# Scores of two attention units in one TensorE stretch, and four PSUM banks for x @ w_in

## Chip, core and metric

One core of a Trainium2 chip runs the whole program in one launch. The metric is the device time in microseconds; the comparison is by the median of several runs.

## The reference

Sliding-window attention with sink tokens, followed by a feed-forward layer with a gate. q, k and v have 4 batches, 8 heads, 768 positions and 64 columns a head. All inputs and the output are float32.

```python
scores = scale * np.matmul(q, k.transpose(0, 1, 3, 2))
keep = is_sink | in_window          # key < 4, or 0 <= query - key < 128
scores = np.where(keep, scores, -1000000000.0)
a = np.exp(scores - max); a = a / (np.sum(a) + 1e-09)
attn = np.matmul(a, v)
x = attn.transpose(0, 2, 1, 3).reshape(3072, 512)
h = x @ w_in                        # 512 -> 2048
g = h * (1.0 / (1.0 + np.exp(-beta * h)))
out = g @ w_out                     # 2048 -> 512
```

## The kernel before

**Attention.** The work is cut into 32 *units*: a unit n is two heads (a pair of heads, 64 columns each, so that both fill the 128 partitions) and half of the 768 queries (384 of them). Four units in a row give one tile of 384 tokens of x, so there are 8 tiles T. `place(n)` gives batch, pair of heads, half, and the buffer set `pb`, which is n % 4. A unit goes through: loads of q, k, v (SP's queue), casts to bf16 (POOL), turning q and k (for units from `XBAR` = 12 on by a DMA transpose on SP's queue, earlier by TensorE), for the second half the sink scores (`scores_sink`, L533 and L536), the scores (TensorE), the exponential (ScalarE), a multiplication with the mask (VectorE), A.V (`attend`, TensorE, L636 and L647, into bank `av`), the normalisation (`normalise`, VectorE, L656 and L658), and the turning of the result into `xT` (`transpose_out`, for units from 12 on a DMA transpose, L667).

Scores are only taken where the window lets something through: six blocks of 128 x 128 per head and unit (`BLOCKS`). The two heads lie in the two halves of the partitions, so each score matmul uses 64 rows of the array, and a matmul of head 0 and one of head 1 run side by side. In units from 12 on `scores_at_once` (L597) takes all six blocks of both heads in one group, head 0 into banks `s0` and `s1`, head 1 into `tr` and `av` (the four banks of `s_ps`); one ScalarE instruction (L604) takes the exponential of all 1536 columns into `E[n % 2]`, one VectorE instruction (L613) masks it.

**Feed-forward.** For each tile T there are 16 groups i of x @ w_in (`hidden`, L695: four matmuls of 384 columns into one bank), each followed by a tanh on ScalarE (`tanh`, L703, into one of three buffers `th`) and by the gate on VectorE (`gate`, L717), which reads the same bank and th and writes `g`. `project` (L744) multiplies g with w_out: 48 matmuls of 512 columns a tile, in three accumulations of 16, into `acc0` and `acc1`, copied out by ScalarE (L752) and stored by SP (L759). `hidden_bank(i)` chooses the bank of a group: before, from i = `S_P0` = 32 on, it alternates between `h0` and `h1`. PSUM has eight banks: h0, h1, s0, s1, tr, av, acc0, acc1.

**Order.** The main loop walks steps s from -6 on. `FIRST[n]` is the step at which unit n starts, and `STEPS` says what happens so many steps later (0: in, 1: sink scores, 3: scores, 5: A.V, 7: out). `casts` and `loads` say at which step the casts and loads of later units are written. In a step there is one group of x @ w_in, three matmuls of w_out, and what the units have there. This program order only fixes who depends on whom: `Prog.order` then places all operations with a list scheduler that has a busy time and a latency for each operation, taking on each engine the one that can start first, and `Prog.emit` writes the order of each engine with the semaphore waits. `P.together` keeps a group of matmuls in one piece; `behind` makes an operation wait for an earlier operation of the same group. So the engines' order follows from the planner, not from the steps directly.

Of the kernel before, what the change touches and what calls it, by code (L numbers as in the profile page):

```python
# [5 lines left out]
F32 = mybir.dt.float32  # L6
AF = mybir.ActivationFunctionType
# [7 lines left out]
SCALE = 1.0 / (D ** 0.5)  # L15
D1 = D + 1

TT = 384
NT = NTOK // TT
NU = 4 * NT  # L20
NM = DF // 128
# [12 lines left out]
BLOCKS = (((0, 0), (0, 1), (0, 2), (2, 2), (1, 1), (1, 2)),  # L34
          ((2, 3), (3, 3), (3, 4), (5, 5), (4, 4), (4, 5)))
# [3 lines left out]
S_P0 = 2 * NM  # L39
# [1 line left out]
S_END = S_PIPE + (NT - 2) * NM  # L41

FIRST = {4: -6, 5: -4, 6: -2, 7: 1, 8: 26, 9: 30, 10: 34, 11: 38}
FIRST.update({12: 44, 13: 47, 14: 50, 15: 53})
FIRST.update({n: 42 + 4 * (n - 12) for n in range(16, NU)})

XBAR, WHOLE = 12, 16

ADDED, FAR = 5, -float(1 << 20)
STEPS = {0: "in", 1: "sink", 2: "a", 3: "b", 5: "av", 7: "out"}  # L50


# [226 lines left out]
def bass_streamingllm_window__then__act_swish_beta_kernel(  # L279
# [25 lines left out]
    def ps(name, shape, dtype):  # L305
        ctx.append(nc.psum_tensor(name, list(shape), dtype))
        return ctx[-1].__enter__()
# [31 lines left out]
    g = [sb(f"g{z}", (128, NM, TT), BF16) for z in range(2)]  # L339
    out_sb = [sb(f"out_sb{z}", (128, NOUT), F32) for z in range(4)]  # L340

    h_ps = ps("h_ps", (128, 2, 512), F32)
    s_ps = ps("s_ps", (128, 4, 512), F32)
    acc = [ps(f"acc{z}", (128, NOUT), F32) for z in range(2)]
    tr_ps, av_ps = s_ps[:, 2, :], s_ps[:, 3, :]

    P = Prog()
    op = P.op


    def pe(n):
        return {"busy": 2.5 + n / 2.4, "lag": 260.0}

    def act(n):
        return {"busy": 80.0 + 0.81 * n, "lag": 140.0}
# [56 lines left out]
    def place(n):  # L412

        return n // 8, n % 4, n // 4 % 2, n % 4
# [115 lines left out]

    def scores_sink(n, bank, name):
        pb = place(n)[3]
        op("pe", lambda e: e.matmul(bank[:, 0, 0:TT], k_sink[pb][:, :], qkT[pb][:, 1, 0, :],  # L533
                                    start=True, stop=True),
           r=[("k_sink", pb), ("qT", pb, 1)], w=[f"{name}0"], **pe(TT))
        op("act", lambda e: e.activation(E_sink[n % 2][:, :], bank[:, 0, 0:TT], AF.Exp, bias=0.0,  # L536
                                         scale=SCALE),
           x=[f"{name}0"], w=[("E_sink", n % 2)], **act(TT))

    def width(half, c):  # L540
        return 128 * sum(t[2] for t in CHUNKS[half][c])
# [41 lines left out]
    def scores_at_once(n):  # L583

        _, _, half, pb = place(n)
        pieces = []
        for x, (kb, qb) in enumerate(BLOCKS[half]):
            if x % 4 and pieces[-1][1] == kb:
                pieces[-1] = (*pieces[-1][:3], pieces[-1][3] + 1)
            else:  # L590
                pieces.append((x, kb, qb, 1))
        with P.together("pe"):
            for x, kb, qb, nq in pieces:
                for hh in range(2):
                    rows = slice(64 * hh, 64 * hh + 64)
                    bank, at = 2 * hh + x // 4, x % 4
                    op("pe", lambda e, kb=kb, bank=bank, qb=qb, at=at, nq=nq, rows=rows: e.matmul(  # L597
                        s_ps[:, bank, 128 * at:128 * (at + nq)],
                        qkT[pb][rows, kb // 3, 1, kb % 3 * 128:kb % 3 * 128 + 128],
                        qkT[pb][rows, half, 0, qb % 3 * 128:(qb % 3 + nq) * 128], start=True, stop=True),  # L600
                       r=[("qT", pb, half), ("qkT", pb, kb // 3)], w=[("s0", "s1", "tr", "av")[bank]],
                       busy=27.0 * nq + 20.0, lag=260.0)
        z = n % 2
        op("act", lambda e: e.activation(  # L604
            E[z][:, :, :, :].rearrange("p c h x -> p c (h x)"),
            s_ps[:, :, :].rearrange("p (h b) x -> p h (b x)", h=2)[:, :, 0:768], AF.Exp,
            bias=0.0, scale=SCALE),
           x=["s0", "s1", "tr", "av"], w=[("E", z, 0), ("E", z, 1)], **act(1536))

    def mask_at_once(n):  # L610
        z, half = n % 2, place(n)[2]
# [72 lines left out]
    def hidden_bank(i):  # L684


        k = i if i < 4 else i % 2 if i < NM else i % 4 if i < S_P0 else 3 - i % 2
        if k < 2:
            return acc[k][:, 0:TT], f"acc{k}"
        return h_ps[:, 3 - k, 0:TT], f"h{3 - k}"  # L690
# [170 lines left out]

    at = {16: 38, 17: 46, 18: 52, 19: 57, 24: 69, 25: 75, 26: 81, 27: 87}
    loads = {t + 2 * x: (n, name) for n, t in at.items() for x, name in enumerate("qkv")}
    casts = {FIRST[n - 2] + 1: n for n in range(6, NU) if n not in (8, 9)}
    for s in range(-6, S_END + NM):
        i = s if 4 <= s < S_P0 else s - NM if S_PIPE <= s < S_END else None
        if i is not None:
            done = hidden(i)
        here = [(n, STEPS[s - FIRST[n]]) for n in range(4, NU) if s - FIRST[n] in STEPS]
        later = []  # L870
        for n, step in here:
            half = place(n)[2]
            if step == "in" and n < XBAR:
                transpose_in(n, eng="dve")
            if step == "sink" and half == 1:
                scores_sink(n, *((h_ps, "h") if n < 8 else (s_ps, "s")))
            if step == "b" and n >= XBAR:
                scores_at_once(n)
                later.append(lambda n=n: mask_at_once(n))
            if step in ("a", "b") and n < XBAR:  # L880
                scores(n, "ab".index(step), *((h_ps, "h") if n < 8 and step == "b" else (s_ps, "s")))
                later.append(lambda n=n, step=step: mask(n, "ab".index(step)))
            if step == "av":
                ended = attend(n)
                later.append(lambda n=n: normalise(n))
                if n >= XBAR:
                    later.append(lambda n=n: transpose_out(n))
                if half == 0:
                    later.append(lambda n=n, ended=ended: sink_keys(n, ended))
            if step == "out":  # L890
                if n < XBAR:
                    transpose_out(n, eng="act" if n < 8 else "dve")
        if s in casts:
            n = casts[s]
            cast(n)
            if n in (12, 13):
                load(n + 2)
        if s == FIRST[5] + 2:
            for x in range(4, 8):
                cast_w(x)  # L900
            load(8)
            load(9)
            load(10)
            load(11)
            load_w(8)
            load_w(9)
            load_w(10)
            load_w(11)
            load_w(12)
            load_w(13)  # L910
            load_w(14)
            load_w(15)
            load(12)
            load(13)
        if s == 34:

            first = {0: (mask_a[:, :], MASK_A), 1: (mask_b[:, 128:512], MASK_B)}
            for half in range(2):
                op("gp", lambda e, half=half: e.tensor_copy(mask_all[:, half, 0:TT], first[half][0]),
                   r=[*first[half][1], ("v_aug", 3, 0)], w=[("mask_all", half, 0)], busy=300.0)  # L920
                for x, n in ((0, 1), (1, 2)):
                    at = TT + 128 * x
                    op("gp", lambda e, half=half, n=n, at=at: e.tensor_copy(
                        mask_all[:, half, at:at + 128 * n], mask_b[:, 0:128 * n]),
                       r=[*MASK_B, ("v_aug", 3, 0)], w=[("mask_all", half, 1)], busy=200.0)
        if s == FIRST[7] + 1:

            for x in (8, 9, 10, 11):
                cast_w(x)
            cast(8)  # L930
            cast_w(12)
            cast_w(13)
            cast(9)
            cast_w(14)
            cast_w(15)
        if S_P0 <= s < S_PIPE:

            for t, (bank, name, eng) in enumerate(
                    ((acc[0][:, :], "acc0", "act"), (acc[1][:, :], "acc1", "act"),
                     (h_ps[:, 1, :], "h1", "dve"))):  # L940
                done = project(0, t, s - S_P0, bank, name, eng)
        elif s >= S_PIPE:
            T = (s - S_PIPE) // NM + 1
            for x in range(3 * (s % NM), 3 * (s % NM) + 3):
                a = (3 * T + x // NM + 1) % 2
                if T == NT - 1 and x // NM == 2:
                    done = project_last(x % NM // 8, x % 8 * 2)
                    done = project_last(x % NM // 8, x % 8 * 2 + 1)
                    continue
                done = project(T, x // NM, x % NM, acc[a][:, :], f"acc{a}")  # L950
        if i is not None:
            gate(i)
        for fn in later:
            fn()
        if s in loads:
            load_whole(*loads[s], done)
# [39 lines left out]
```

## Time and profile before

| | |
|---|---|
| median of 3 runs | 229.04 us (228.92 to 229.59) |
| the profiled execution, its time | 229.57 us |
| its span, first to last instruction | 227.8 us |
| granted TensorE clock, mean | 0.999 |
| TensorE matmuls (PE) | 217.5 us busy, 1709 records |
| ScalarE (ACT) | 139.7 us busy |
| VectorE (DVE) | 135.8 us busy |
| GpSimd (POOL) | 76.7 us busy |
| w_out matmuls, 128x512 (L744 into acc) | 380 ns each, 329 records |
| w_in matmuls, 128x384 (L695 into h_ps) | 326 ns each, 424 records |
| exponential of a unit (L604) | 1444 ns, 20 of them |
| mask of a unit (L613) | 996 ns, 20 of them |
| tanh (L703), gate (L717) | 581 and 552 ns |

The profile tells of one execution. Matmuls are pipelined: the duration of a matmul (326 ns for 384 columns) is longer than the time from its start to the start of the next one, and it is the latter that adds up on TensorE. PEld are the weight loads of TensorE, which overlap its matmuls. In lists of groups and of waits, the time behind "<-" says what ended the idle time; "issue" is idle time for which the profile shows no releaser. L-numbers are lines of the kernel before, unless they are said to be of the changed one.

### The profile page before, as it was taken

To read this page: it belongs to the slowest core of one execution; us is meant where nothing else is said; L and a number is where in the kernel's file an instruction comes from. 1 tells how busy PE (TensorE), PEld (TensorE's weight loads), DVE (VectorE), ACT (ScalarE), POOL (GpSimd) and SP (SyncE) were. 2 spreads that over 40 slices of the span, in tenths; PEclk is the share of its full clock that TensorE was granted. 3 is DMA by queue.
4 is the path that set the end of the run, shared out by engine and by line. 5 is a ranking of instruction groups with operands and counts; after the bars stand their busy time and mean duration, and the time that the engine had idled before them with its cause. 6 is when DMAs were issued, how large, how long until landed. Compare 5 with 4: busy or idle time off the path is not lost.

```text
span 227.8 us, 4408 instructions
## 1 busy us (share of the span) xinstructions
PE 217.5 (95%) x1709; PEld 120.4 (53%) x1733; DVE 135.8 (60%) x261; ACT 139.7 (61%) x222; POOL 76.7 (34%) x149
## 2 busy tenths in 40 slices
PE   7897898999999999999999999999999999999995
PEld 4554555655445555444555555555555555555554
DVE  5657887798666656534677577656656555353300
ACT  2765987794436667536777676665676764555410
POOL 6877776798434130653204266000000000000000
PEclk9999999999999999999999999999999999999999
DMA  6999999996999989999999998501101101111022
GB/s 190 295 351 300 338 320 270 353 370 158 135 215 279 207 174 210 288 231 147 243 239 207 264 211 168 134 20 63 46 20 63 63 20 63 46 49 46 12 80 92
DMA packets 95436, 39.78 MB, mean 175 GB/s; under 512 B 81960, under 2 KB 88376, under 8 KB 95416
## 3 DMA queue, kind: packets, MB, share of 16 engines
q1 hardware_dynamic: 93760, 38.75, 67.5%
q10 hardware_dynamic: 1656, 0.76, 1.2%
q8 instruction: 13, 0.21, 0.4%
q14 instruction: 7, 0.06, 0.1%
HBM read 27.30 MB, written 6.29 MB: 147 GB/s over the span
## 4 chain that ended last, share of the span: by engine, by line
PE 88%; DVE 6%; DMA 2%; issue 1%; ACTq 1%; ACT 1%; DVEq 0%
PE acc L744 34%; PE h_ps L695 30%; PE s_ps L647 5%; PE acc L695 4%; PE s_ps L597 4%; DMA g<-in_v_dram 2%; DVE qkT L513 2%; PE s_ps L560 2%; PE h_ps L744 1%; DVE E L578 1%; PE s_ps L636 1%; PE s_ps L504 1%; DVE g L717 1%; DVE o_norm L658 1%; PE s_ps L533 1%
## 5 line engine op out<-in xcount | busy, mean ns | idle before, releaser
L744 PE MATMUL acc<-w_out,g 128*128 128x512 bf16 x329 | 89.3, 380 | 1.2 <-issue 0.3
L703 ACT ACTIVATE th<-h_ps,beta_half 128x384 f32<-128x384 f32 x106 | 60.5, 581 | 46.7 <-PE h_ps L695 43.8
L695 PE MATMUL h_ps<-xT,w_in 128*128 128x384 bf16 x424 | 82.2, 326 | 0.1
L717 DVE SCALAR_TENSOR_TENSOR g<-th,h_ps 128x384 bf16<-128x384 f32 x106 | 57.6, 552 | 39.8 <-ACT th L703 38.2
L695 PEld LDWEIGHTS h_ps<-xT,w_in 128*128 128x128 bf16 x424 | 40.5, 98 | 32.7 <-DVE g L717 1.8
L744 PEld LDWEIGHTS acc<-w_out,g 128*128 128x128 bf16 x352 | 32.1, 98 | 30.1 <-issue 3.7
L613 DVE TENSOR_TENSOR E<-E,mask_all 128x1536 bf16<-128x1536 bf16 x20 | 19.9, 996 | 18.6 <-ACT E L604 18.6
L604 ACT ACTIVATE E<-s_ps 128x1536 bf16<-128x1536 f32 x20 | 28.9, 1444 | 3.0 <-PE s_ps L597 2.9
L484 POOL CAST v_aug<-v_stage 128x384 bf16<-128x384 f32 x32 | 18.3, 586 | 29.6 <-PE s_ps L647 15.3
L481 POOL CAST qk<-q_stage 128x384 bf16<-128x384 f32 x32 | 18.2, 569 | 19.0 <-DMA q_stage<-in_q_dram 13.4
L481 POOL CAST qk<-k_stage 128x384 bf16<-128x384 f32 x31 | 17.7, 570 | 11.8 <-DMA k_stage<-in_k_dram 11.7
L647 PEld LDWEIGHTS s_ps<-v_aug,E 128*128 128x128 bf16 x384 | 17.1, 97 | 5.6 <-DVE E L613 0.7
L752 ACT ACTIVATE out_sb<-acc 128x512 f32<-128x512 f32 x22 | 13.0, 596 | 11.0 <-PE acc L744 10.6
L647 PE MATMUL s_ps<-v_aug,E 128*128 128x65 bf16 x384 | 19.3, 193 | 0.3 <-DVE E L578 0.3
L658 DVE TENSOR_TENSOR o_norm<-s_ps,rden 128x384 bf16<-128x384 f32 x32 | 17.8, 558 | 1.6
L567 ACT ACTIVATE E<-s_ps 128x768 bf16<-128x768 f32 x16 | 13.0, 810 | 9.2 <-PE s_ps L560 9.2
L695 PE MATMUL acc<-xT,w_in 128*128 128x384 bf16 x88 | 17.0, 327 | 1.2 <-DVE g L717 1.2
L703 ACT ACTIVATE th<-acc,beta_half 128x384 f32<-128x384 f32 x22 | 12.7, 583 | 6.0 <-PE acc L695 5.4
L717 DVE SCALAR_TENSOR_TENSOR g<-th,acc 128x384 bf16<-128x384 f32 x22 | 11.5, 549 | 3.1 <-ACT th L703 2.8
L695 PEld LDWEIGHTS acc<-xT,w_in 128*128 128x128 bf16 x88 | 7.9, 98 | 6.6 <-DVE g L717 2.0
L656 DVE RECIPROCAL rden<-s_ps 128x6 f32<-128x6 f32 x32 | 6.1, 191 | 7.0 <-PE s_ps L647 6.7
L597 PE MATMUL s_ps<-qkT 64*128 64x256 bf16 (+2 forms) x144 | 10.1, 254 | 0.0
(77 smaller groups left out, 158.9 us busy)
## 6 DMA issues: line engine op xcount, KB each, us to landing
out_dram<-out_sb SPq DMA_DIRECT2D x23, 256.0 KB, 2.4
wst<-in_moe_w_in_dram SPq DMA_DIRECT2D x8, 512.0 KB, 5.3
wst<-in_moe_w_out_dram SPq DMA_DIRECT2D x8, 512.0 KB, 9.0
q_stage<-in_q_dram SPq DMA_DIRECT2D x8, 384.0 KB, 4.1
k_stage<-in_k_dram SPq DMA_DIRECT2D x8, 384.0 KB, 3.9
v_stage<-in_v_dram SPq DMA_DIRECT2D x8, 384.0 KB, 3.8
v_stage<-in_v_dram SPq DMA_DIRECT2D x30, 96.0 KB, 4.6
q_stage<-in_q_dram SPq DMA_DIRECT2D x12, 192.0 KB, 5.1
```

The source lines that it names most:

```text
L481: op(eng, lambda e, x=x, name=name: e.tensor_copy(qk16[z][:, x, :, :, :], view(name)), r=[(name + "_stage", pb, half, hh) for hh in range( ...
L484: op("gp", lambda e: e.tensor_copy(v_aug[pb][:, 3 * half:3 * half + 3, :, 0:D], view("v")), r=[("v_stage", pb, half, hh) for hh in range(2 ...
L567: op("act", lambda e: e.activation(E[n % 2][:, c, :, 0:at], bank[:, 0:2, 0:at], AF.Exp, bias=0.0, scale=SCALE), x=[f"{name}0", f"{name}1"] ...
L597: op("pe", lambda e, kb=kb, bank=bank, qb=qb, at=at, nq=nq, rows=rows: e.matmul(s_ps[:, bank, 128 * at:128 * (at + nq)], qkT[pb][rows, kb ...
L604: op("act", lambda e: e.activation(E[z][:, :, :, :].rearrange("p c h x -> p c (h x)"), s_ps[:, :, :].rearrange("p (h b) x -> p h (b x)", h ...
L613: op("dve", lambda e: e.tensor_tensor(both, both, mask_all[:, half, :].unsqueeze(1).to_broadcast([128, 2, 768]), ALU.mult), r=[("E", z, 0) ...
L647: last=(x == len(kbs) - 1): e.matmul(av_ps[:, at + hh * D1:at + hh * D1 + D1], E[z][:, c, h2, col:col + 128], v_aug[pb][:, kb, hh, :], sta ...
L658: op("dve", lambda e: e.tensor_tensor(o_norm[o][:, :, :, :].rearrange("p m h d -> p (m h) d"), src[:, :, 0:D], rden[z][:, :].unsqueeze(2). ...
L695: return op("pe", lambda e: e.matmul(bank, w_in16[:, c, m * 128:(m + 1) * 128], xT[:, c, T * TT:(T + 1) * TT], start=(c == 0), stop=(c == 3)),
L703: op("act", lambda e: e.activation(th[i % 3][:, :], bank, AF.Tanh, bias=0.0, scale=beta_half[:, m:m + 1]), x=[name], r=["beta"], w=[("th", ...
L717: op("dve", lambda e: e.scalar_tensor_tensor(g[T % 2][:, m, :], th[i % 3][:, :], 1.0, bank, ALU.add, ALU.mult), r=[("th", i % 3)], x=[name ...
L744: node = op("pe", lambda e: e.matmul(bank, g[T % 2][:, m, t * 128:(t + 1) * 128], w_out16[:, m, :], start=(m == 0), stop=(m == NM - 1)), r ...
```

## The change

From unit 16 on (`PAIRED`) units n and n + 1, n even, take their scores in one group, `scores_pair`: the six banks h0, h1, s0, s1, tr, av are now one tensor `six`; unit n has av, h0, h1 and unit n + 1 has s0, s1, tr, each with 12 blocks of 128 columns in three banks without holes (before: 6 blocks in each pair of banks). The middle bank of the three holds blocks of both heads, and the first matmul of head 1 there is made to wait (`behind`) for the last one of head 0 there. The matmuls of both units and both heads are interleaved so that the columns given to each head stay even. Two exponentials and two masks follow. The A.V of the second unit comes `LATE` = 2 steps later, casts of odd units too; both units of a pair start at the same step, pairs 8 steps apart.

The groups of x @ w_in go round h0, h1, s0, s1 from i = 32 on (`TURN` = 0). In a step that holds sink scores or scores of a unit from 12 on, the gate is written ahead of them, since it still reads a bank that they may write. The sink scores of the second half go to `s0` for units 8 to 15 as before and to `tr` for units from 16 on.

```diff
@@ -41,12 +41,14 @@
 S_END = S_PIPE + (NT - 2) * NM
 
 FIRST = {4: -6, 5: -4, 6: -2, 7: 1, 8: 26, 9: 30, 10: 34, 11: 38}
-FIRST.update({12: 44, 13: 47, 14: 50, 15: 53})
-FIRST.update({n: 42 + 4 * (n - 12) for n in range(16, NU)})
+FIRST.update({12: 44, 13: 47, 14: 50, 15: 53, 16: 60, 17: 60})
+FIRST.update({n: 68 + 8 * (n // 2 - 9) for n in range(18, NU)})
+TURN = 0
 
 XBAR, WHOLE = 12, 16
 
 ADDED, FAR = 5, -float(1 << 20)
+LATE, PAIRED = 2, 16
 STEPS = {0: "in", 1: "sink", 2: "a", 3: "b", 5: "av", 7: "out"}
 
 
@@ -339,8 +341,8 @@
     g = [sb(f"g{z}", (128, NM, TT), BF16) for z in range(2)]
     out_sb = [sb(f"out_sb{z}", (128, NOUT), F32) for z in range(4)]
 
-    h_ps = ps("h_ps", (128, 2, 512), F32)
-    s_ps = ps("s_ps", (128, 4, 512), F32)
+    six = ps("six", (128, 6, 512), F32)
+    s_ps, h_ps = six[:, 0:4, :], six[:, 4:6, :]
     acc = [ps(f"acc{z}", (128, NOUT), F32) for z in range(2)]
     tr_ps, av_ps = s_ps[:, 2, :], s_ps[:, 3, :]
 
@@ -530,12 +532,12 @@
 
     def scores_sink(n, bank, name):
         pb = place(n)[3]
-        op("pe", lambda e: e.matmul(bank[:, 0, 0:TT], k_sink[pb][:, :], qkT[pb][:, 1, 0, :],
+        op("pe", lambda e: e.matmul(bank[:, 0:TT], k_sink[pb][:, :], qkT[pb][:, 1, 0, :],
                                     start=True, stop=True),
-           r=[("k_sink", pb), ("qT", pb, 1)], w=[f"{name}0"], **pe(TT))
-        op("act", lambda e: e.activation(E_sink[n % 2][:, :], bank[:, 0, 0:TT], AF.Exp, bias=0.0,
+           r=[("k_sink", pb), ("qT", pb, 1)], w=[name], **pe(TT))
+        op("act", lambda e: e.activation(E_sink[n % 2][:, :], bank[:, 0:TT], AF.Exp, bias=0.0,
                                          scale=SCALE),
-           x=[f"{name}0"], w=[("E_sink", n % 2)], **act(TT))
+           x=[name], w=[("E_sink", n % 2)], **act(TT))
 
     def width(half, c):
         return 128 * sum(t[2] for t in CHUNKS[half][c])
@@ -607,6 +609,46 @@
             bias=0.0, scale=SCALE),
            x=["s0", "s1", "tr", "av"], w=[("E", z, 0), ("E", z, 1)], **act(1536))
 
+    def scores_pair(n):
+
+        banks = {n: ("av", "h0", "h1"), n + 1: ("s0", "s1", "tr")}
+        with P.together("pe"):
+            runs = {0: [], 1: []}
+            for hh in range(2):
+                for bank in ((1, 0) if hh == 0 else (2, 1)):
+                    for u in banks:
+                        for x, (kb, qb) in enumerate(BLOCKS[place(u)[2]]):
+                            if (6 * hh + x) // 4 != bank:
+                                continue
+                            if runs[hh] and runs[hh][-1][:3] == [u, bank, kb]:
+                                runs[hh][-1][5] += 1
+                            else:
+                                runs[hh].append([u, bank, kb, qb, (6 * hh + x) % 4, 1])
+            columns, middle = [0, 0], {}
+            while runs[0] or runs[1]:
+                hh = 0 if runs[0] and (not runs[1] or columns[0] <= columns[1]) else 1
+                u, bank, kb, qb, at, nq = runs[hh].pop(0)
+                columns[hh] += nq
+                _, _, half, pb = place(u)
+                rows = slice(64 * hh, 64 * hh + 64)
+                op("pe", lambda e, kb=kb, bank=bank + (3 if u == n else 0), qb=qb, at=at, nq=nq, rows=rows,
+                   pb=pb, half=half: e.matmul(
+                    six[:, bank, 128 * at:128 * (at + nq)],
+                    qkT[pb][rows, kb // 3, 1, kb % 3 * 128:kb % 3 * 128 + 128],
+                    qkT[pb][rows, half, 0, qb % 3 * 128:(qb % 3 + nq) * 128], start=True, stop=True),
+                   r=[("qT", pb, half), ("qkT", pb, kb // 3)], w=[banks[u][bank]],
+                   behind=middle.pop(u, None) if (hh, bank) == (1, 1) else None,
+                   busy=27.0 * nq + 2.0, lag=260.0)
+                if (hh, bank) == (0, 1):
+                    middle[u] = len(P.group.items) - 1
+            P.group.busy += 200.0
+        for u, names in banks.items():
+            first = 3 if u == n else 0
+            op("act", lambda e, u=u, first=first: e.activation(
+                E[u % 2][:, :, :, :].rearrange("p c h x -> p (c h x)"),
+                six[:, first:first + 3, :].rearrange("p b x -> p (b x)"), AF.Exp, bias=0.0, scale=SCALE),
+               x=names, w=[("E", u % 2, 0), ("E", u % 2, 1)], **act(1536))
+
     def mask_at_once(n):
         z, half = n % 2, place(n)[2]
         both = E[z][:, :, :, :].rearrange("p c h x -> p c (h x)")
@@ -684,7 +726,10 @@
     def hidden_bank(i):
 
 
-        k = i if i < 4 else i % 2 if i < NM else i % 4 if i < S_P0 else 3 - i % 2
+        if i >= S_P0:
+            k = (i + TURN) % 4
+            return (h_ps[:, k, 0:TT], f"h{k}") if k < 2 else (s_ps[:, k - 2, 0:TT], f"s{k - 2}")
+        k = i if i < 4 else i % 2 if i < NM else i % 4
         if k < 2:
             return acc[k][:, 0:TT], f"acc{k}"
         return h_ps[:, 3 - k, 0:TT], f"h{3 - k}"
@@ -861,22 +906,32 @@
 
     at = {16: 38, 17: 46, 18: 52, 19: 57, 24: 69, 25: 75, 26: 81, 27: 87}
     loads = {t + 2 * x: (n, name) for n, t in at.items() for x, name in enumerate("qkv")}
-    casts = {FIRST[n - 2] + 1: n for n in range(6, NU) if n not in (8, 9)}
+    casts = {FIRST[n - 2] + (3 if n % 2 and n - 2 >= PAIRED else 1): n for n in range(6, NU) if n not in (8, 9)}
     for s in range(-6, S_END + NM):
         i = s if 4 <= s < S_P0 else s - NM if S_PIPE <= s < S_END else None
         if i is not None:
             done = hidden(i)
-        here = [(n, STEPS[s - FIRST[n]]) for n in range(4, NU) if s - FIRST[n] in STEPS]
+        here = [(n, STEPS[s - FIRST[n]]) for n in range(4, NU)
+                if s - FIRST[n] in STEPS and not (n >= PAIRED and n % 2 and STEPS[s - FIRST[n]] == "av")]
+        here += [(n, "av") for n in range(PAIRED + 1, NU, 2) if s - FIRST[n] == 5 + LATE]
         later = []
+        if i is not None and i >= S_P0 and any(n >= XBAR and step in ("sink", "b") for n, step in here):
+            gate(i)
+            i = None
         for n, step in here:
             half = place(n)[2]
             if step == "in" and n < XBAR:
                 transpose_in(n, eng="dve")
             if step == "sink" and half == 1:
-                scores_sink(n, *((h_ps, "h") if n < 8 else (s_ps, "s")))
-            if step == "b" and n >= XBAR:
+                scores_sink(n, *((h_ps[:, 0, :], "h0") if n < 8 else (s_ps[:, 0, :], "s0") if n < PAIRED
+                                 else (tr_ps, "tr")))
+            if step == "b" and XBAR <= n < PAIRED:
                 scores_at_once(n)
                 later.append(lambda n=n: mask_at_once(n))
+            if step == "b" and n >= PAIRED and n % 2 == 0:
+                scores_pair(n)
+                later.append(lambda n=n: mask_at_once(n))
+                later.append(lambda n=n: mask_at_once(n + 1))
             if step in ("a", "b") and n < XBAR:
                 scores(n, "ab".index(step), *((h_ps, "h") if n < 8 and step == "b" else (s_ps, "s")))
                 later.append(lambda n=n, step=step: mask(n, "ab".index(step)))
```

## The prediction

> **What bounds the kernel now.** I read the page first (busy shares, slices, the chain that ended last), then the list of waits for TensorE, then the timeline of TensorE around one unit's scores, and last the timelines of ScalarE and VectorE around one exponential. The page:
>
> ```profile
> PE 217.5 (95%) x1709; PEld 120.4 (53%) x1733; DVE 135.8 (60%) x261; ACT 139.7 (61%) x222; POOL 76.7 (34%) x149
> PE   7897898999999999999999999999999999999995
> PEclk9999999999999999999999999999999999999999
> PE 88%; DVE 6%; DMA 2%; issue 1%; ACTq 1%; ACT 1%; DVEq 0%
> ```
>
> TensorE is busy in nine tenths or more of every slice from the eighth on (about 40 us), at full clock, and the chain that ended last is 88% TensorE. VectorE and ScalarE are busy 60% of the time. So what counts is what TensorE executes and where it stands still. The waits of TensorE and of its weight loads:
>
> ```profile
> PE acc L809 <- DVE v_aug L369: 1.3, 1, 1.3
> PE acc L695 <- DVE g L717: 1.2, 2, 0.8
> ...
> PEld s_ps L597 <- issue: 6.1, 18, 0.4
> PEld acc L744 <- issue: 3.7, 23, 0.2
> ```
>
> No wait of the matmuls for another engine is over 1.3 us in all, and those two lie in the first 40 us. The longest entry of the weight loads is L597, the scores of units 12 to 31, with "issue" as its reason: 18 times about 0.34 us in which no engine was waited for. The timeline shows what that is (matmuls, then weight loads):
>
> ```profile
> 115.91 1.46 PE L695 MATMUL h_ps<-xT,w_in 128*128 128x384 bf16 x8
> 117.30 0.50 PE L597 MATMUL s_ps<-qkT 64*128 64x128 bf16 x8
> 117.74 0.61 PE L744 MATMUL acc<-w_out,g 128*128 128x512 bf16 x2
> 118.18 1.46 PE L695 MATMUL h_ps<-xT,w_in 128*128 128x384 bf16 x8
> 119.48 0.33 PE L533 MATMUL s_ps<-qkT,k_sink 128*128 128x384 bf16 x1
> 117.30 0.28 PEld L597 LDWEIGHTS s_ps<-qkT 64*128 64x128 bf16 x8 [0.32 <-issue]
> 117.73 0.11 PEld L744 LDWEIGHTS acc<-w_out,g 128*128 128x128 bf16 x2 [0.16 <-issue]
> ```
>
> Eight L695 in front of a full-array matmul take 119.48 - 118.18 = 1.30 us from start to start, 0.1625 each. The same eight in front of scores take 117.30 - 115.91 = 1.39: **0.09 us are lost going in**. The stretch itself lasts 117.74 - 117.30 = 0.44. Its two heads run side by side on 64 rows each, 768 columns a head, and 768 columns take 2 x 0.1625 = 0.325; of the other 0.115 about 0.02 goes to the joints of four pieces, and **about 0.095 are lost coming out**. Both weight-load lines agree: inside full-array work weights are loaded ahead, and here the first load on either side comes only with its matmul. So one unit's scores cost 0.53 us, of which 0.19 is the change from whole array to half arrays and back.
>
> **The change, part by part.** (1) *Stretches.* Units 16 to 31 were 16 stretches and become 8 pairs; in the changed program's instruction order each pair's score matmuls (its L635) do stand together, with full-array work on both sides. Units 12 to 15 keep theirs. Before, per pair: 2 x 0.53 = 1.06. After: in 0.09, columns 4 x 0.1625 = 0.65, out 0.095, joints about 0.025 (14 or 18 matmuls instead of 12 or 16, because a unit lies on three banks instead of four and one more run of blocks is cut at a bank's edge). Sum 0.86. Gain 0.20 a pair, 8 x 0.20 = **1.6 us**, all on the path.
>
> (2) *Uneven sides.* Before, both heads always ran pieces of equal width. Now widths alternate (256 for one head beside 128 and 128 for the other, and so on). If each half starts its next piece when it is free, adding up widths in issue order gives 0.66 for the longer side against 0.64 ideal; that is in the sum. No trace row shows unequal neighbours. From below: nothing gained over 0.64 (8 x 0.02 = 0.16 better). From above: see the second rival.
>
> (3) *TensorE waits for itself*, twice a pair, as the middle bank is written by one head and then by the other. The awaited matmul is among the first five of the stretch; a 256-wide score matmul is 269 ns long (by its form, in the groups), so it ends 0.27 and 0.38 after the stretch's start (its start at 0 or 0.11), while the waiting ones are due at 0.44 and 0.55. Covered by 0.17, taken at nothing. Behind each wait are queued the last one to five score matmuls and then the projections. If the cover were gone, each wait would cost the part of a matmul beyond its streaming, 0.269 - 0.107 = 0.16, 2.6 us for all 16; the row nearest to that is L533 right after, which also has a semaphore wait in front of it and starts with no loss. I keep 0 to 0.05 each for the range.
>
> (4) *Two exponentials and two masks back to back.* ScalarE and VectorE:
>
> ```profile
> 144.60 1.45 ACT L604 ACTIVATE E<-s_ps 128x1536 bf16<-128x1536 f32 x1
> 145.95 1.04 ACT L703 ACTIVATE th<-h_ps,beta_half 128x384 f32<-128x384 f32 x2
> 146.08 0.96 DVE L613 TENSOR_TENSOR E<-E,mask_all 128x1536 bf16<-128x1536 bf16 x1 [0.97 <-ACT E L604]
> 146.96 1.01 DVE L717 SCALAR_TENSOR_TENSOR g<-th,h_ps 128x384 bf16<-128x384 f32 x2
> ```
>
> ScalarE's next instruction starts 1.35 after an exponential's start, VectorE's next 0.88 after a mask's. Count from the first projection behind a pair (t = 0). The first unit's exponential runs from 0 to 1.45, the second to 2.80; the masks end at 2.5 and 3.8; reciprocal and normalisation of the first unit (0.29 from start to start, then 0.56) end at 4.7. TensorE's order in pair 16/17: thirteen projections (0.216 each, 2.81), first A.V (0.36), eight projections (1.73), second A.V at 4.9. So slack 0.3 and 0.2. In pair 18/19 eight projections (1.73) stand before x @ w_in may write banks h0 and h1, which the first exponential frees at 1.5; two groups of it follow and the first A.V starts at 3.0 (mask 2.5); VectorE then has two gates before the reciprocal, normalised at 5.5, second A.V at 6.0. The other pairs repeat these two patterns. All of it fits, but with 0.1 to 0.5 of slack where before an A.V had one exponential ahead of it. I charge 0.1 us in all for slips; the trace of before shows one of 0.13, at an A.V.
>
> (5) *Ring of four banks for x @ w_in.* From unit 12 on (hidden group 32) it takes h0, h1, s0, s1 instead of h0, h1. It must not write s0 or s1 between a unit's scores and its exponential, and scores must wait for the gate (L717) that reads one last, so this gate is issued ahead of the scores. In the order x @ w_in often comes as eight groups in a row (5.2 us). A group every 0.65 needs a tanh (0.47 to 0.58) and a gate (0.46 to 0.55) each: both keep up, and a bank is free about 1.5 us after its group, against 1.95 until it comes round. Nothing charged. In units 13 to 15 I followed each wait in the new order (gate before the sinks of unit 15: free 0.6 before it is wanted): nothing.
>
> (6) *Moved steps.* The second unit's A.V, normalisation and output transpose come 2 steps later, casts of odd units too, and on SP's queue the output transposes of a pair follow each other with loads of later units behind them (k of unit 26, the q/k transposes of 24 and 25 start about 2 us later than before). They are wanted 20 us after. Output transposes of unit 23, the tightest, land about 3 us ahead of the first x @ w_in that reads them. Nothing charged. Units 0 to 11 are as before, and so is the drain behind the last matmul.
>
> Sum: 229.57 (the profiled execution: span 227.8 and 1.8 around it) - 1.6 + 0.1 = 228.07. That execution is 0.53 above the median of the runs, 229.04; on the median: **227.5 us**.
>
> **The rivals.** *Chain behind a pair too long* (slower). Place: the A.V of both units. If ScalarE comes to the first exponential one tanh late (0.58), everything in (4) shifts by 0.58 against slacks of 0.3 and 0.2: waits of 0.28 and 0.1 more, some 0.38 a pair, 3.0 us, which is 229.0 - 1.6 + 3.0 = 230.4. It decides from 0.2 us of waiting a pair on. For it: slacks are that small. Against: ScalarE is 61% busy, and in the order it stands free when the scores end, except for at most one output copy.
>
> *Halves that keep step* (no change). If a piece may not end before the piece issued ahead of it in the other half, the narrow ones are held; adding up the order of a pair in this way gives 0.80 for its columns instead of 0.66, 8 x 0.14 = 1.1 us back: 228.6. For it: every pair of the old trace ends together, as equal widths must. Against: pieces in the old trace follow with no more than a joint, so a half does not wait for the array to empty. The Trainium skill, "TensorE: Matmul & The Clock Gate", Part 3, says that matmuls are in order in start and in end; read strictly it gives this rival's time, and no run here shows it, as all neighbours have been equal so far.
>
> *More than the drains* (faster still): the larger blocks also remove small slips that TensorE has today. By the busy sums of windows from 68 to 217 us it is idle 149.0 - 147.85 = 1.15 us there; half of that gone gives 226.9.
>
> That the change does not do what it says is excluded by the order.
>
> **Numbers.** Forecast 0.65, chain too long 0.14, keep step 0.15, more 0.06. A measurement of this kernel tells 0.3%, 0.7 us, from no change: faster is below 228.35, slower above 229.7. Faster 0.65 + 0.06, same 0.15 + 0.01, slower 0.13. The range takes the forecast, the other end of (3) (16 x 0.05 = 0.8 more), keep step, and of the long chain only its edge: 226.8 to 229.2.
>
> **What would show it.** Right: 12 stretches of half-array scores, from the first start to the next full-array matmul 0.77 for a pair, 0.09 lost in front of it; TensorE's waits as short as now. Wrong: a pair of 0.9 or more (keep step, or the own waits); an entry of A.V waiting for a mask or a normalisation above 0.5 us in all; x @ w_in waiting for a gate; a wait for an output transpose.

## The result, and the profile after

| | before | changed |
|---|---|---|
| median | 228.94 us (228.12 to 230.1, 20 runs) | 227.19 us (226.59 to 229.17, 20 runs) |
| the profiled execution, its time and span | 229.57, 227.8 us | 227.53, 225.7 us |

The ratio is 0.9924, 95% interval 0.9908 to 0.994: 1.75 us faster. The forecast was 227.5 us. From here on L-numbers are lines of the changed kernel, unless said otherwise (scores of a pair L635, w_out L789, w_in L740, A.V L689 and L678, exponential L647, mask L655, normalisation L698 and L700, gate L762).

The page of the changed kernel: busy time and share of each engine, TensorE in 40 slices, the chain that ended last.

```profile
PE 216.1 (96%) x1729; PEld 122.5 (54%) x1749; DVE 134.3 (60%) x261; ACT 141.9 (63%) x222; POOL 75.1 (33%) x149
PE   7997888999999999999999999999999999999995
PE 83%; DVE 11%; DMA 2%; ACT 1%; issue 1%; ACTq 1%; DVEq 0%
```

TensorE is still what bounds it. The larger share of VectorE in the chain lies in its first 53 us, ahead of the change. The list of waits of TensorE and its weight loads (in all, times, longest):

```profile
PE acc L854 <- DVE v_aug L371: 1.3, 1, 1.3
PE acc L740 <- DVE g L762: 1.2, 2, 0.8
...
PEld six L635 <- issue: 2.1, 5, 0.4
```

The entry that led the list before, 18 late weight loads at the scores of units 12 to 31 (6.1 us), is now five at a pair's scores, with three more there put down to a gate; the four stretches that stay single (units 12 to 15) have entries of their own. No wait of a matmul for a mask, a normalisation or a bank behind a pair has joined the list. Now the stretch itself, in the timeline of TensorE around the pairs of units 18 and 20:

```profile
110.72 0.59 PE L789 MATMUL acc<-w_out,g 128*128 128x512 bf16 x2
111.24 0.83 PE L635 MATMUL six<-qkT 64*128 64x256 bf16 x14
112.01 1.90 PE L789 MATMUL acc<-w_out,g 128*128 128x512 bf16 x8
...
121.61 0.84 PE L635 MATMUL six<-qkT 64*128 64x256 bf16 x18
122.38 2.98 PE L789 MATMUL acc<-w_out,g 128*128 128x512 bf16 x13
```

From the first score to the next full-array matmul a pair takes 112.01 - 111.24 = 0.77 us. In the raw starts (the trace's start times in whole nanoseconds) all eight take 0.766 to 0.772, with 0.095 to 0.097 lost in front; the four stretches of units 12 to 15 that stay single take 0.435 to 0.437 behind the same 0.096. So a pair is 0.096 + 0.769 = 0.865 against 2 x (0.096 + 0.436) = 1.064: **0.199 us a pair, 1.59 us for eight**.

To see whether this is all, I measured from the first score of unit 12 to the first matmul of the last tile's own code (L770): 153.52 us before, 151.64 after, 1.88 less. Of the 0.29 beyond 1.59, 0.19 are two short waits at A.V that the trace of before has (0.126 at 107.97 us and 0.065 at 136.72, over the normal distance from start to start) and the trace of after has not. Another 0.08 belong to the stretches: the first full-array matmul behind each is followed by the next one 0.010 us later than elsewhere, in both traces, and there are 12 stretches now where there were 20. So a pair saves 0.209 in all, 1.67 for eight. The last 0.02 or 0.03 I cannot place. On the two profiled executions the span fell by 2.16; the other 0.28 lie ahead of unit 12's scores, where the orders agree. That part is not steady: in the kernels run here in which unit 12 stays single its first score falls anywhere from 66.9 to 68.0 us. By the medians 1.75 us are gained (1.4 to 2.1 by the interval of the ratio); the 1.67 of the stretches lie within that with the 0.19 of the waits or without.

### The profile page after: what moved, and what is told of

It is laid out like the page before. It is cut to its first block, busy times and chain, and to the rows that moved or that the text cites. A ratio compares the mean times of both kernels' runs of the same rounds, so it can differ in the third digit from the quotient of the medians.

```text
span 225.7 us, 4502 instructions
## 1 busy us (share of the span) xinstructions
PE 216.1 (96%) x1729; PEld 122.5 (54%) x1749; DVE 134.3 (60%) x261; ACT 141.9 (63%) x222; POOL 75.1 (33%) x149
## 4 chain that ended last, share of the span: by engine, by line
PE 83%; DVE 11%; DMA 2%; ACT 1%; issue 1%; ACTq 1%; DVEq 0%
PE acc L789 34%; PE six L740 29%; PE six L689 5%; DVE g L762 4%; PE six L635 3%; PE acc L740 2%; DVE qkT L515 2%; DMA g<-in_v_dram 2%; DVE E L580 2%; PE six L562 2%; PE six L789 1%; PE six L535 1%; PE six L678 1%; ACT th L748 1%; DVE o_norm L700 1%
## 5 line engine op out<-in xcount | busy, mean ns | idle before, releaser
L789 PE MATMUL acc<-w_out,g 128*128 128x512 bf16 x333 | 84.4, 379 | 1.0 <-DVE g L762 0.2
L748 ACT ACTIVATE th<-six,beta_half 128x384 f32<-128x384 f32 x106 | 61.0, 581 | 31.9 <-PE six L740 26.8
L740 PE MATMUL six<-xT,w_in 128*128 128x384 bf16 x424 | 78.2, 326 | 0.1
L762 DVE SCALAR_TENSOR_TENSOR g<-th,six 128x384 bf16<-128x384 f32 x106 | 57.3, 551 | 29.8 <-ACT th L748 27.0
L740 PEld LDWEIGHTS six<-xT,w_in 128*128 128x128 bf16 x424 | 40.3, 98 | 29.2 <-ACT E L606 0.7
L789 PEld LDWEIGHTS acc<-w_out,g 128*128 128x128 bf16 x352 | 32.7, 98 | 33.7 <-issue 2.0
L655 DVE TENSOR_TENSOR E<-E,mask_all 128x1536 bf16<-128x1536 bf16 x20 | 19.6, 979 | 28.6 <-ACT E L647 23.3
L647 ACT ACTIVATE E<-six 128x1536 bf16<-128x1536 f32 x16 | 22.3, 1448 | 9.4 <-PE six L635 9.3
L569 ACT ACTIVATE E<-six 128x768 bf16<-128x768 f32 x24 | 18.7, 810 | 9.8 <-PE six L562 9.8
L689 PE MATMUL six<-v_aug,E 128*128 128x65 bf16 x384 | 19.4, 193 | 0.5 <-DVE E L580 0.5
L689 PEld LDWEIGHTS six<-v_aug,E 128*128 128x128 bf16 x384 | 17.2, 97 | 4.8 <-DVE E L580 0.8
L700 DVE TENSOR_TENSOR o_norm<-six,rden 128x384 bf16<-128x384 f32 x32 | 17.8, 557 | 1.4
L740 PE MATMUL acc<-xT,w_in 128*128 128x384 bf16 x88 | 17.0, 327 | 1.2 <-DVE g L762 1.2
L762 DVE SCALAR_TENSOR_TENSOR g<-th,acc 128x384 bf16<-128x384 f32 x22 | 11.5, 549 | 3.1 <-ACT th L748 2.8
L740 PEld LDWEIGHTS acc<-xT,w_in 128*128 128x128 bf16 x88 | 7.9, 98 | 6.6 <-DVE g L762 2.0
L471 POOL CAST w_in<-wst 128x1024 bf16<-128x1024 f32 x8 | 8.3, 1040 | 6.1 <-DMA wst<-in_moe_w_in_dram 6.1
```

What stands on the lines that cost most here:

```text
L569: op("act", lambda e: e.activation(E[n % 2][:, c, :, 0:at], bank[:, 0:2, 0:at], AF.Exp, bias=0.0, scale=SCALE), x=[f"{name}0", f"{name}1"] ...
L647: op("act", lambda e, u=u, first=first: e.activation(E[u % 2][:, :, :, :].rearrange("p c h x -> p (c h x)"), six[:, first:first + 3, :].re ...
L655: op("dve", lambda e: e.tensor_tensor(both, both, mask_all[:, half, :].unsqueeze(1).to_broadcast([128, 2, 768]), ALU.mult), r=[("E", z, 0) ...
L689: last=(x == len(kbs) - 1): e.matmul(av_ps[:, at + hh * D1:at + hh * D1 + D1], E[z][:, c, h2, col:col + 128], v_aug[pb][:, kb, hh, :], sta ...
L700: op("dve", lambda e: e.tensor_tensor(o_norm[o][:, :, :, :].rearrange("p m h d -> p (m h) d"), src[:, :, 0:D], rden[z][:, :].unsqueeze(2). ...
L740: return op("pe", lambda e: e.matmul(bank, w_in16[:, c, m * 128:(m + 1) * 128], xT[:, c, T * TT:(T + 1) * TT], start=(c == 0), stop=(c == 3)),
```

## The experiments

I went in with this theory: the gain is the eight round trips between the whole array and its halves, and nothing behind a pair takes any of it back. The rivals: the ring of four banks brings it, the size of the stretch does not matter, or the chain behind a pair takes back part. Kernels of one chip were compared with the kernel before on that chip; ratios are to it. Where I speak of a "wait at" a matmul, it is the time from the previous matmul's start beyond the columns of that matmul.

**The ring of four banks alone** (all units as before, x @ w_in round four banks):

```
-FIRST.update({12: 44, 13: 47, 14: 50, 15: 53, 16: 60, 17: 60})
-FIRST.update({n: 68 + 8 * (n // 2 - 9) for n in range(18, NU)})
+FIRST.update({12: 44, 13: 47, 14: 50, 15: 53})
+FIRST.update({n: 42 + 4 * (n - 12) for n in range(16, NU)})
-LATE, PAIRED = 2, 16
+LATE, PAIRED = 2, NU
```

> The changed kernel with no pairs: all units from 12 on take their scores alone, at the steps of before; only the ring of four banks for x @ w_in (and the gate written ahead of the scores) is left. Theory 1, the gain is the eight saved trips into half-array work at 0.19 us and joints: 20 stretches of 0.44 us again, nothing of the 1.6 us is left, at most the 0.3 us of small slips: 228.6 to 229.0 us against 228.9 before. Theory 2, the gain comes from the ring, which frees TensorE from gates: about 227.2 us, as the changed kernel.

229.04 us, ratio 1.0019 (0.9995 to 1.0043). The ring by itself brings nothing. Its trace says the same: from unit 12's first score to the last tile's own code it takes 153.46 us, before 153.52. It has neither of the two waits at A.V that before has, and one of 0.17 at 125.69 us, behind a single stretch, for an output copy.

**Pairs, but x @ w_in on two banks:**

```
-            k = (i + TURN) % 4
+            k = i % 2
```

> The changed kernel with x @ w_in on h0 and h1 alone, as before; the pairs stay. Theory 1: the eight trips are saved as well; groups of x @ w_in can no longer come eight in a row at full rate (two banks, about 1.5 us from a group's end to its free bank, so at most one group in 1.1 us), the planner puts projections between; 227.2 to 227.6 us, pairs at 0.77 us from first score to next full-array matmul. Theory 2: without the ring TensorE waits for gates next to each pair, 0.2 us or more a pair: 228.5 us or more.

232.57 us, ratio 1.0166 (1.0138 to 1.0194): 3.8 us slower than before. The pairs are as short as in the change (0.765 to 0.772), so the trips are saved, and 1.6 + 3.8 = 5.4 us are lost elsewhere. TensorE's waits in this kernel, from 92 to 200 us:

```profile
PE six L740 <- ACT E L647: 1.4, 2, 1.0
PE acc L789 <- ACT out_sb L797: 1.1, 2, 0.9
PE six L535 <- ACT E_sink L538: 0.7, 1, 0.7
PE six L535 <- issue: 0.4, 1, 0.4
PE six L740 <- DVE g L762: 0.2, 1, 0.2
```

They add up to 3.8 us of standing still, and to 5.1 us counted from start to start. The first is new. The first unit of a pair has its scores in h0 and h1, and these are now the only banks for x @ w_in. In the timeline (TensorE, ScalarE):

```profile
124.33 0.84 PE L635 MATMUL six<-qkT 64*128 64x256 bf16 x18
125.10 0.61 PE L789 MATMUL acc<-w_out,g 128*128 128x512 bf16 x2
125.15 2.79 ACT L647 ACTIVATE E<-six 128x1536 bf16<-128x1536 f32 x2 [1.65 <-PE six L635]
126.74 1.46 PE L740 MATMUL six<-xT,w_in 128*128 128x384 bf16 x8 [1.04 <-ACT E L647]
```

Behind the pair stand two projections, and then x @ w_in waits 1.04 us until the first exponential has read h0 and h1. On four banks thirteen projections stand there (122.38 in the fence of the result). So my theory was right on what is saved and too narrow on what is needed: the ring brings nothing alone, and without it a pair costs more than it saves. The waits of w_in for an exponential make 1.2 and 0.56 us of the 5.1 in this way of counting; whether the rest (sinks, w_out, gates) follows from them was not tested one by one. The steps at which units start were kept as chosen for four banks, so that two banks with other steps would do better is not excluded.

**One more trip in the middle of each pair, and a control.** An extra matmul of 128 columns, once over all 128 rows and once over 64 rows, at the same place in the pair:

```
+                if sum(columns) >= 12 and not put:
+                    put = True
+                    op("pe", lambda e: e.matmul(spare, ident[0:128, :], ones[0:128, 0:128], ...))   # control: [0:64]
```

> The changed kernel with one more matmul in the middle of each pair's scores: 128 columns over the whole array, into a place that a later score matmul overwrites, so the result does not change; the order of everything else is the same. Theory 1: each costs its 0.056 us of streaming and one more trip out of half-array work and back, 0.19: 0.245 a pair, 2.0 us in all, 229.2 us; a pair takes 1.01 us instead of 0.77. Theory 2 (the trips are not what is paid): 0.056 a pair, 0.45 us, 227.6 us.

> The control of the split: the same extra matmul of 128 columns in the same place of the order, but on 64 rows, one half of the array, so TensorE stays in half-array work; the result does not change. Both theories: at most its streaming, 0.055 us a pair and less if the other half hides it: 227.2 to 227.6 us, a pair at 0.77 to 0.83 us. If it costs 0.2 us a pair like the full one, an extra piece in the stretch is dear in itself and theory 1 falls.

Over all rows: 230.26 us, ratio 1.0064 (1.0041 to 1.0087). Control: 227.70 us, 0.9943 (0.9923 to 0.9962). The difference is 2.56 us, 0.32 a pair. The timeline of the one over all rows (the extra matmul is L634, scores L642 and w_out L796 in both kernels):

```profile
95.46 0.55 PE L642 MATMUL six<-qkT 64*128 64x256 bf16 x7
95.94 0.23 PE L634 MATMUL six<-ones,ident 128*128 128x128 bf16 x1
96.11 0.55 PE L642 MATMUL six<-qkT 64*128 64x128 bf16 x7
96.59 2.76 PE L796 MATMUL acc<-w_out,g 128*128 128x512 bf16 x12
```

and of the control:

```profile
94.63 0.61 PE L642 MATMUL six<-qkT 64*128 64x256 bf16 x9
95.02 0.22 PE L634 MATMUL six<-ones,ident 64*128 64x128 bf16 x1
95.08 0.43 PE L642 MATMUL six<-qkT 64*128 64x128 bf16 x5
95.44 0.82 PE L796 MATMUL acc<-w_out,g 128*128 128x512 bf16 x3
```

From first score to w_out: 1.13 to 1.14 us in the raw starts of all eight pairs against 0.81 to 0.82. The same matmul costs 0.05 on half the rows and 0.37 on all of them. In the raw starts the extra matmul begins 0.484 us into the pair. The last score of one half, 384 columns, starts at 0.229 and streams for 0.160, so 0.095 pass between its last column and the extra matmul, as at the end of a pair. From that one's last column to the next score pass 0.11, the 0.096 of every way in and the 0.010 behind a stretch's first full-array matmul. That is 0.20, the trip as forecast. The rest of the 0.32, about 0.12, I had left out: at that point the halves are uneven, one has run dry at 0.29 and the other at 0.39, and the change of mode makes the first wait for the second (behind the extra matmul the same happens again, at 0.29 and 0.39). At the end of an uncut pair the halves run dry within 0.01 of each other (with 14 matmuls at 0.610 + 0.053 and 0.565 + 0.107). The Trainium skill, "TensorEngine Tiling (Array Packing)", Key Properties, says that changing the tiling mode drains TensorE; the trace agrees, and gives it a size: 0.095 out, 0.096 to 0.11 in, and on top, here, 0.12 for halves that differ by 0.10.

**The chain behind a pair, delayed.** One needless ScalarE copy of 384 columns ahead of the two exponentials, all orders kept:

```
+        op("act", lambda e: e.activation(junk[:, :], w_in16[:, 0, 0:TT], AF.Copy, ...),
+           r=[*banks[n], ("w_in", 0)], w=["junk"], busy=0.0, lag=0.0)
```

> The kernel after the change, but behind each pair of scores ScalarE first does one needless copy of 384 columns (its nearest rows: about 0.5 to 0.58 us) and only then the two long exponentials; every engine's order stays. All that follows a pair (two exponentials, two masks, two o_norms, the banks that come free) is about 0.5 us later. It measures how much room lies behind a pair, and what the rival 'chain too long' costs. In the trace of the changed kernel the first A.V is ready 0.33 us and the second 0.30 us before TensorE comes to it, in the pair of units 16 and 17. My theory (the chain fits, with 0.2 to 0.3 us to spare): TensorE then waits 0.2 to 0.3 us at each pair, 1.6 to 2.4 us in all, so 228.8 to 229.7 us, with waits for VectorE's masks, for o_norm or for ScalarE's exponential ahead of A.V or x @ w_in. The recorded rival's price (0.38 a pair) would put it at 230.2 us or above. If there is far more room than I read, it stays at 227.0 to 227.6 us.

229.24 us, ratio 0.9994 (0.9974 to 1.0015), the whole gain is gone. Pair of units 16 and 17 (here L636 scores, L792 w_out, L650 exponential, L692 A.V):

```profile
95.58 2.98 PE L792 MATMUL acc<-w_out,g 128*128 128x512 bf16 x13
95.63 0.52 ACT L646 ACTIVATE junk<-w_in 128x384 bf16<-128x384 bf16 x1 [1.64 <-PE six L636]
96.06 2.77 ACT L650 ACTIVATE E<-six 128x1536 bf16<-128x1536 f32 x2
98.54 0.42 PEld L692 LDWEIGHTS six<-v_aug,E 128*128 128x128 bf16 x12 [0.47 <-DVE E L658]
100.93 0.42 PEld L692 LDWEIGHTS six<-v_aug,E 128*128 128x128 bf16 x12 [0.62 <-DVE o_norm L703]
```

The copy shifts the exponentials by 0.43 us. TensorE then waits 0.145 for the mask and 0.298 for the normalisation at this pair (a part of the second is a mask that took 1.24 instead of 0.96 here), and 0.23 at each of the pairs 18, 22, 26 and 30, where x @ w_in waits for the banks of the first exponential. In all the traced waits make 1.89 us, 0.24 a pair; by the ratios it is 0.007 x 229 = 1.6 us. So there are about 0.2 us of room at x @ w_in (0.43 - 0.23) and 0.3 at the first A.V (0.43 - 0.145). My forecast of 1.6 to 2.4 us held.

**Pairs from unit 12, and from unit 14:**

```
-FIRST.update({12: 44, 13: 47, 14: 50, 15: 53, 16: 60, 17: 60})
+FIRST.update({12: 46, 13: 46, 14: 53, 15: 53, 16: 60, 17: 60})   # PAIRED = 12
+FIRST.update({12: 44, 13: 47, 14: 52, 15: 52, 16: 60, 17: 60})   # PAIRED = 14
```

> The same pairing, begun at unit 12 instead of 16: two more pairs, two more round trips between the whole array and its halves saved. If a trip is worth 0.197 us wherever it is saved, the time falls by 0.39 us below the changed kernel's: 226.8 us, ratio to before about 0.990. If there is no room in the first half for the longer chain behind a pair (there x @ w_in is still in its earlier part and the loads are not all done), TensorE waits there and it gives 227.2 to 228.5 us instead.

> The same pairing, begun at unit 14: one pair more, one round trip more saved, 0.197 us below the changed kernel, 227.0 us, ratio to before about 0.9915, if nothing waits. Begun at unit 12 it saved two trips and lost 0.84 us to waits of TensorE, most of it for masks and o_norm behind the pair of units 16 and 17, whose place among the projections had shifted. If the same shift comes with this one pair, there are again 0.3 to 0.8 us of waits there, and it gives 227.3 to 228.0 us.

From 12: 227.82 us, ratio 0.9942 (0.9921 to 0.9963). From 14: 227.41 us, 0.9941 (0.9919 to 0.9963). Neither beats the change (0.9924); the two intervals overlap with its own, and the traces decide. The new pairs are as short as the others, 0.77. From 12, TensorE waits 0.84 us more than in the change (0.167, 0.249 and 0.264 of it behind the pair of units 16 and 17), against 0.39 saved: 0.45 worse, by the ratios 0.41. From 14 it waits 0.52 more behind the pair of unit 20, against 0.2 saved: 0.32 worse, by the ratios 0.39. Timeline of the latter:

```profile
121.43 0.84 PE L635 MATMUL six<-qkT 64*128 64x256 bf16 x18
122.20 2.33 PE L789 MATMUL acc<-w_out,g 128*128 128x512 bf16 x10
123.73 0.96 DVE L655 TENSOR_TENSOR E<-E,mask_all 128x1536 bf16<-128x1536 bf16 x1 [2.64 <-ACT E L647]
...
124.75 0.29 PE L689 MATMUL six<-v_aug,E 128*128 128x65 bf16 x4 [0.16 <-DVE E L655]
```

Ten projections stand between scores and A.V, in the change thirteen at this pair, and the A.V that needs the mask starts 124.75 - 121.43 = 3.32 us behind the pair's first score. In the kernel with pairs from 12 a waiting A.V started 3.31 behind it. That is what the chain needs. In the change the planner puts 3.58 there or more; in these two it puts 3.0 and 3.1 at one pair (3.32 and 3.31 less the waits of 0.32 and 0.167). So the room of 0.3 us is not a reserve that the planner keeps: it comes out of how many projections happen to stand there.

**The second A.V earlier:**

```
-LATE, PAIRED = 2, 16
+LATE, PAIRED = 0, 16   # and, in another kernel, 1
```

> The changed kernel, but the second unit of a pair has its A.V in the same step as the first (two steps earlier than in the change). The bank for A.V is freed by the first unit's o_norm 4.6 us after the pair's first score, and the second mask ends at 3.6 us. Theory (the second A.V stands at the place where its operands have just come, so the two steps are needed): unless the planner fills in as many projections, TensorE waits up to 1 us at some pairs, 228 to 230 us. If the planner moves projections ahead of the second A.V by itself, it is 227.0 to 227.6 us, and the two steps matter for nothing.

> The changed kernel with the second unit's A.V one step earlier instead of two later than the first's plus two (its delay is one step, not two). In the planned order this moves it ahead of one group of four x @ w_in (0.65 us) in the two patterns in which eight or sixteen x @ w_in stand there (the pairs of units 18, 22, 26 and 30); in the others nothing moves. In the changed kernel's trace the first unit's o_norm ends 0.54 us before that A.V. Theory (the room behind a pair is a few tenths, and the two steps are needed): 0.1 us of wait at each of the four pairs if the A.V could start the moment o_norm ends, 0.3 us if about 0.2 us lies between the end of o_norm and the A.V, so 0.4 to 1.3 us more than the changed kernel, 227.6 to 228.5 us. If the delay does not matter: 227.0 to 227.4 us.

With no delay: 228.75 us, 0.9983 (0.9964 to 1.0002). This run does not answer its question. Both A.V of a pair are then written ahead of the first normalisation and into the same bank, so the first unit's result is lost and the dependence that I meant to test is not in it. With one step: 227.39 us, 0.9919 (0.9895 to 0.9944), and the trace has one wait that the change has not, 0.04 us at the second A.V of units 16 and 17, whose mask took 1.24 us here. I expected 0.4 to 1.3 us of loss. I had misread which pairs move: the planner moved the second A.V at units 25 and 29 only, by one group of w_in, from 7.4 and 6.7 to 6.76 and 6.1 us behind the first score; at the pair of unit 16 in the change 5.67 are enough (100.84 - 95.17). At the two pairs where it changes anything, one step of delay is as good as two.

## Why the prediction was right

It was right in sign and mechanism, and in size to a few tenths of a microsecond; that these tenths partly cancel is luck (see the sum).

1. *Stretches.* Forecast 0.20 a pair and 1.6 us; measured 0.199 and 1.59, with the 0.010 behind a stretch 0.209 and 1.67, and the 0.77 named as the sign of it is there in all eight pairs. The extra trip of the third experiment shows the cost from the other side.
2. *Uneven sides*, and the rival "halves that keep step" (0.80 for the columns, 228.6 us). Refuted in the raw starts. In the pair of unit 18 the first pieces are 256 wide in one half (start 0) and 128 in the other (start 0.003); by the program's order the narrow half starts its next pieces at 0.070 and 0.126, the wide one at 0.120. No half was held. The Trainium skill, "TensorE: Matmul & The Clock Gate", Part 3, says that matmuls are in order in start and in end; the starts are in order here, but a half that takes up its next piece at 0.070, while the piece issued ahead in the other half streams until 0.11, is against the strict reading of the ends. The Trainium skill, "TensorEngine Tiling (Array Packing)", Key Properties, says that tiles operate independently, and the trace agrees with that.
3. *TensorE's waits for itself.* Taken at nothing. In the same pair the two awaiting matmuls start at 0.456 and 0.565, where the step has them due (0.44 and 0.55), and the pair is no longer for them. The upper end, 0.8 us, is ruled out.
4. *Two exponentials and two masks.* The order of events was as forecast. Room at the first A.V: forecast 0.3, found 0.28 (3.58 - 3.3) behind a mask of 0.96 us. At x @ w_in: forecast 1.73 - 1.5 = 0.23, found 0.2. At the second A.V: forecast 0.2, found 0.24 (normalised at 100.54, A.V at 100.84 us, and 0.06 lie between the two where A.V waits, with the delayed chain). The term that was off is the charge on top: **+0.1 us for slips; in the trace it was -0.2**, as the two waits that A.V had before are gone and no new one came. They stood behind masks that took 1.27 and 1.26 us instead of 0.96. The first, from the trace of before (its mask is L613, its cast L481):

```profile
106.60 0.50 POOL L481 CAST qk<-q_stage 128x384 bf16<-128x384 f32 x1 [3.85 <-DMA qkT<-qk]
106.65 1.27 DVE L613 TENSOR_TENSOR E<-E,mask_all 128x1536 bf16<-128x1536 bf16 x1 [0.79 <-ACT E L604]
```

The mask ends at 107.92, and the A.V that needs it starts late, at 107.97. A GpSimd cast was running when the mask began. That is the pattern in all eleven traces kept: 22 of their 220 masks took 1.05 to 1.31 us, and these 22, and no others, began while a cast still had 0.24 us or more to run; each took longer by that remainder less about 0.15 us. So, as far as the traces show, these slips hang on where a cast happens to fall, and not on the size of the blocks.

5. *Ring of four banks.* TensorE loses no time at x @ w_in from 68 us on. The charge of nothing was right, but "nothing" hid that the pairs need the ring: 5.4 us without it, at the same steps.
6. *Moved steps.* TensorE loses no time to an output transpose or a cast from 68 us on.

*The sum.* From the profiled execution it gave 228.07; the profiled execution after took 227.53. The 0.54 between are the slips (0.3), the first 68 us (0.28) and the 0.08 behind the stretches, less 0.12 by which the time around the span was longer this time (227.53 - 225.68 against 229.57 - 227.84). Only the 0.08 belong to the mechanism; the first 68 us vary from kernel to kernel. The step to the median, -0.53, was -0.34 this time (227.53 to 227.19). So 227.54 came within 0.35 of 227.19 with errors of both signs in it, and part of that agreement is luck.

*The chain too long* did not happen, and its price was sound: for 0.58 of delay it had 0.38 a pair, the fifth experiment measured 0.24 for 0.43. The margin is as thin as it said: those 0.43 us eat the whole gain.

*More than the drains* saw that slips might go (0.2 us did), but not by larger blocks: the ring alone, with single stretches, has neither of the two waits either. And it was built on a wrong reading: its 1.15 us of idle TensorE are missing records. In the groups of the changed kernel:

```profile
L789 PE MATMUL acc<-w_out,g 128*128 128x512 bf16 x333 | 84.4, 379 | 1.0 <-DVE g L762 0.2
L789 PEld LDWEIGHTS acc<-w_out,g 128*128 128x128 bf16 x352 | 32.7, 98 | 33.7 <-issue 2.0
```

352 weight loads and 333 matmuls: 19 matmul records are not there, and each leaves a gap of 0.052 us or a little more in which TensorE seems idle (the weight loads show the matmul that is not listed). From 68 to 217 us there are 17 such gaps in the trace of after, 0.89 us, all that it calls idle; in that of before there are nineteen, and one of 0.158 us right behind a stretch of scores, 1.15 us, again all of it. The slips that did go, 0.2 us, were never in this idle time: they are shorter than the modelled end of the matmul before them.

## What to carry to other kernels

Where row-tiled matmuls stand between full-array ones, count the stretches, not the matmuls: each cost about 0.2 us here on top of its columns, so joining two saves that much, provided both halves run dry at the same moment. Joining them doubles the softmax work that comes at once and the banks that are held; price the wait of the next writer of those banks, and of the first reader of the results, in tenths of a microsecond, before counting the gain. And compare weight loads with matmuls in the list of groups before taking short idle times for waits.

## What the runs showed that I had not expected

- A full-array matmul in the middle of a stretch costs more than the trip, when the halves have uneven work before it: 0.32 us instead of 0.20.
- A ScalarE copy of 384 columns, 0.52 us long, delays the exponentials behind it by 0.43 only.
- The mask of 1536 columns takes 0.96 us as a rule, and up to 1.31 when it begins while a GpSimd cast is running (the second mask of units 16 and 17 with the delayed chain, and with pairs from 12, took 1.24 and 1.25). The traces show the two together each time; no experiment moved a cast.
- The first full-array matmul behind a stretch of half-array scores is followed 0.010 us later than elsewhere, on top of what is lost going in and coming out.
